# Attention and token mixing: the second batch in written order, with all sums of weights in it

## The chip, the cores and the metric

The kernel runs on one core of a Trainium2 chip. The metric is the device time of one execution in microseconds; of several runs the median is taken. A core has five engines that each work through their own instructions in order: PE (matmuls into PSUM), DVE, ACT and POOL (element-wise work) and SP (here it only issues DMAs). An instruction waits on semaphores for what other engines or DMAs have to finish, and while it waits, nothing behind it on its engine runs.

## The reference, cut to what matters

The first half is a clustered attention over 4 batches, 8 heads, 768 positions and a head size of 64. Its result, one matrix x of 768 x 512 per batch, goes through a token-mixing layer:

```python
def _moe_ref(x, w_theta, w_tok_r, w_tok_i, w_ch):
    theta = x @ w_theta
    cos_t, sin_t = (np.cos(theta), np.sin(theta))
    zr = x * cos_t
    zi = x * sin_t
    yr = np.einsum('ts,bsd->btd', w_tok_r, zr)
    yi = np.einsum('ts,bsd->btd', w_tok_i, zi)
    y = yr + yi
    u = x + y
    return (u + np.maximum(u @ w_ch, 0.0)).astype(np.float32)
```

All is float32. The change touches the token mixing alone, with one exception in the attention's last part.

## The kernel before

**Precision.** Matmuls of the second half take each operand as a pair: a high part (a cast on ACT, `nc.scalar.copy` into a float32r tile) and a low part (the value minus its high part, on POOL or DVE). A product is three matmuls: high by high, high by low, low by high.

**Tiles and stages.** A batch has NT = 6 tiles of 128 tokens; n = 6 b + t counts them over all batches. For each tile: `theta_parts` (L931) loads columns of x and makes `xh`, `xl`; `theta_angle` (L940) does the 12 matmuls of the angle into `tp`; `theta_turn` (L947) reduces the angle on DVE (`rotation_reduce`, L662), takes its absolute value on ACT, and transposes a block of x into `xn` on DVE (`rotation_turn`, L651, which also loads the next block `xb`); two sines on ACT (L986 or L965); two products with `xn` on DVE; then the pair `z`.

**Two ways to mix.** Batches 0 and 1 (b < `PLAIN` = 2) use `mix` (L1018), the plain products with `w_r[t]`, `w_i[t]` into `y`. `z` tiles come from the pool `mz` with two buffers. Batches 2 and 3 use `mix_forms` (L1107): seven products of sums of `z` with sums of weights, in place of the plain ones. The 7 x 6 = 42 sums of weights are made on the chip by `make_forms` (L1048). For a tile t it loads the raw weights into `spares[0]` and `spares[1]`; for each of the seven, DVE adds two parts (five of the seven; two are a part as it is), ACT casts to the high half and POOL subtracts to the low half of one of only two buffers, `spares[2]` and `spares[3]`, and SP stores the buffer to DRAM (`w_f`). `load_forms` (L1069) brings the sums back into tiles where the plain weights lay (`PLACE`, L1044). `forms[0]` lies in the four `spares` and in parts of `w_r[0]`, `w_i[0]`.

**Channel layer.** `channel_plain` (L1176) follows each plain batch: `add_y` (L1148) adds `y` to x on DVE, splits it on ACT (`uh`) and POOL (`ul`), and 96 matmuls with `w_c` (L1165) give the output.

**Order.** Up to the end of the attention and from `begin` (L1229) on, `in_order` (L689) ties each engine's instructions to the order in which they are written. Between these two, which before holds all of batches 0 and 1, the compiler's scheduler orders each engine by the program's priority and its own timing. There the loop at L1203 runs, per tile, `theta` of n + 2 (`AHEAD`), `mix` of n, and five or six steps of `make_forms`. From batch 2 on the steps are written out by hand: `done` (products with `xn`), `angle`, `before` (parts), the mixing, `turn`.

`behind(x)` (L628) places an instruction after x on its engine. In the attention, units u = 0 to `NUT` - 1 = 191 each end in exponentials on ACT (`exps`, L481).

Of the kernel before, what the change touches and what calls it, by code (L numbers as in the profile page):

```python
# [9 lines left out]
F32 = mybir.dt.float32  # L10
# [31 lines left out]
def kernel(  # L42
# [218 lines left out]
    def f(ap):  # L261
        return ap.bitcast(F32)
# [218 lines left out]
    def exps(u, j):  # L481

        pi, a, i = split_u(u)
        s = st[pi]
        last_exp[0] = nc.scalar.activation(out=s["at", a, i][:, j], in_=s["sc", j], func=AF.Exp, scale=SCALE)  # L485

    def add_exps(u):
# [108 lines left out]
    def run(gen):  # L596
        for _ in gen:
            pass
# [16 lines left out]
        first.update(rab=rab, xn=xn)  # L615

    first, first_sin = {}, [None]

    def rotation_tiles(n, name):
        pool = ma[n % 2]  # L620
# [7 lines left out]
    def behind(x):  # L628
        return tc.issue_after(x.ins) if x is not None else nullcontext()
# [240 lines left out]
    def u_tile(name):  # L870
        return m2.tile([P, NCT, HS], F32R, tag="u", name=name, bufs=4)
# [24 lines left out]
    def late():  # L896

        for t in range(EARLY, NT):
            for w, x in ((w_r, "r"), (w_i, "i")):
                hi, lo = w[t]  # L900
                kept = u_tile("kept").rearrange("p c s -> p (c s)").bitcast(F32)[:, 0:S]
                nc.sync.dma_start(out=kept, in_=w_d[t, x])
                with behind(weights_after[0]):
                    nc.scalar.copy(out=hi, in_=kept)
                nc.gpsimd.tensor_tensor(out=lo, in0=kept, in1=f(hi), op=ALU.subtract)
            if t == NT - 2:
                yield
        for c in range(NCT):
            for gen in split_w(*w_c[c], w_ch[c * P:(c + 1) * P], DM, wt_pair, nc.gpsimd, CK):
                run(gen)  # L910
            yield
# [8 lines left out]
    def load_columns(n):  # L920

        b, t = divmod(n, NT)
        if 0 < b < B and n not in columns:
            columns[n] = mxs.tile([P, NCT, P], F32, tag="xs", name=f"xs{n}")
            with tc.issue_after(last_load[0].ins):
                nc.sync.dma_start(out=columns[n], in_=xT_d[b][:, :, t * P:(t + 1) * P])
# [4 lines left out]
    def theta_parts(n, eng, after=None):  # L931
        b, t = divmod(n, NT)
        load_columns(n + 1)
        xs = columns.pop(n) if b else xts[b][:, :, t * P:(t + 1) * P]
        turning[n] = xh, xl, xn, kk, rab = rotation_tiles(n, f"{b}_{t}")
        nc.scalar.copy(out=xh, in_=xs)
        with behind(after):
            eng.tensor_tensor(out=xl, in0=xs, in1=f(xh), op=ALU.subtract)

# [12 lines left out]
    def theta(b, t):  # L952
        n = b * NT + t
        late = n == AHEAD
        theta_parts(n, nc.vector, last_out[0] if late else None)
        theta_angle(n, last_rows[0] if late else last_mix[0] if n == AHEAD + 1 else None)
        theta_turn(n)
        xh, xl, xn, kk, rab, tp = turning.pop(n)
        rotate(b, t, rab, xn)
# [7 lines left out]
    def turned(n):  # L967

        xh, xl, xn, kk, rab, tp = turning.pop(n)
        b, t = divmod(n, NT)  # L970
        for x in (1, 0):
            nc.vector.tensor_tensor(out=rab[:, x], in0=rab[:, x], in1=xn, op=ALU.mult)  # L972
        keep_turned(b, t, rab)

    def keep_turned(b, t, rab):
        zs[b, t] = rab
        z_d[b, t] = dram.tile([P, 2, DM // 2], F32, tag=f"z{t}", name=f"zd{b}_{t}", bufs=2)
        nc.sync.dma_start(out=z_d[b, t], in_=rab[:, :, DM // 2:DM])
# [39 lines left out]
    def mix(b, t):  # L1018
        for d in range(NCT):
            for w, (zh, zl) in zip((w_r[t], w_i[t]), zs[b, t]):  # L1020
                for zz, ww in ((zh, w[0]), (zh, w[1]), (zl, w[0])):
                    first = t == 0 and w is w_r[0] and zz is zh and ww is w[0]
                    last = t == NT - 1 and w is w_i[t] and zz is zl
                    for c0, c1, lead in cuts(d):
                        last_mix[0] = nc.tensor.matmul(  # L1025
                            y_at(d, c0, c1), lhsT=zz[:, d * P:(d + 1) * P], rhs=ww[:, c0:c1],
                            start=first and lead, stop=last, skip_group_check=True)
# [19 lines left out]

    def make_forms():  # L1048

        for t in range(NT):  # L1050
            for x, k in enumerate("ri"):
                with behind(last_mix[0]):
                    nc.sync.dma_start(out=f(spares[x]), in_=w_d[t, k])
            part = [f(spares[x])[:, c:c + HS] for x in range(2) for c in (0, HS)]
            yield
            for x, m in enumerate(ORDER):
                to = spares[2 + (7 * t + x) % 2]
                hi, lo = to[:, 0:HS], to[:, HS:S]
                p, op, q = W_SUM[m]
                src = part[p]  # L1060
                if op is not None:
                    src = mzb.tile([P, 2, HD], F32, tag="zb", name=f"sum{t}_{m}").rearrange("p x n -> p (x n)")[:, 0:HS]
                    nc.vector.tensor_tensor(out=src, in0=part[p], in1=part[q], op=op)
                nc.scalar.copy(out=hi, in_=src)  # L1064
                nc.gpsimd.tensor_tensor(out=lo, in0=src, in1=f(hi), op=ALU.subtract)  # L1065
                nc.sync.dma_start(out=w_f[t][:, m - 1], in_=f(to))
                yield

    def load_forms(t, ms=ORDER):  # L1069
        for m in ms:  # L1070
            nc.sync.dma_start(out=f(forms[t][m]), in_=w_f[t][:, m - 1])
# [76 lines left out]
    def add_y(b, c0, c1):  # L1148

        xT, n = xts[b], c1 - c0  # L1150
        uh, ul = (u_tile(f"u{x}{b}_{c0}")[:, :, 0:n] for x in "hl")
        for d in range(NCT):
            x = xT[:, d, c0:c1]
            for n0, n1, _ in cuts(d, c0, c1):
                nc.vector.tensor_tensor(
                    out=xT[:, d, n0:n1], in0=y_at(d, n0, n1), in1=xT[:, d, n0:n1], op=ALU.add)
            nc.scalar.copy(out=uh[:, d, :], in_=x)
            nc.gpsimd.tensor_tensor(out=ul[:, d, :], in0=x, in1=f(uh[:, d, :]), op=ALU.subtract)  # L1158
        return uh, ul
# [9 lines left out]
    def channel_out(b, e, ch, cp):  # L1169
        c = slice(ch * HS, (ch + 1) * HS)  # L1170
        ot = m2.tile([P, HS], F32, tag="ot", name=f"ot{b}_{ch}_{e}", bufs=2)
        nc.vector.scalar_tensor_tensor(
            out=ot, in0=cp, scalar=0.0, in1=xts[b][:, e, c], op0=ALU.max, op1=ALU.add)
        nc.sync.dma_start(out=out[b, e * P:(e + 1) * P, c], in_=ot)

    def channel_plain(b):  # L1176
        us = [add_y(b, ch * HS, (ch + 1) * HS) for ch in range(2)]
        for x in range(2 * NCT):
            ch, e = divmod(x, NCT)
            cp = (mbank(f"cp{b}_{x}") if x < 2 else y[x - 2])[:, 0:HS]  # L1180
            channel_products(cp, e, us[ch], range(NCT))
            channel_out(b, e, ch, cp)

    def channel(b, us):
        EARLY_GROUPS = 5
# [13 lines left out]

    rotate(0, 0, first["rab"], first["xn"])  # L1200
    theta(0, 1)
    late_weights, new_forms = late(), make_forms()
    for n in range(PLAIN * NT):  # L1203
        b, t = divmod(n, NT)
        theta(*divmod(n + AHEAD, NT))
        if b == 0:
            weights_after[0] = splits[n + 1]
            next(late_weights, None)
        mix(b, t)
        if 0 < n < PLAIN * NT - 1 and t < NT - 1:  # L1210
            for _ in range(5 if b == 0 else 6):
                next(new_forms, None)
        if b == PLAIN - 1:
            if t == NT - 2:
                run(new_forms)
            if t > 2:
                load_columns(n + AHEAD + 2)
            if t == NT - 2:
                load_forms(0)
            if t > 2:  # L1220
                load_forms(t - 2)
        if t == NT - 1:
            channel_plain(b)
            load_x(b + 1)
    us = [u_tile(f"u{x}") for x in range(4)]
    forms[4] = {
        m: us[x // 2].rearrange("p c s -> p (c s)")[:, x % 2 * S:(x % 2 + 1) * S] for x, m in enumerate(ORDER)}
    four[0] = pm[1].tile([P, 512], F32, tag="bank", name="four")
    begin = len(nc.cur_bb.bb.instructions)  # L1229

    last = B * NT

    def before(n):
        if n < last:
            theta_parts(n, nc.gpsimd)

    def angle(n):
        if n < last:
# [7 lines left out]
    def done(n):  # L1246
        if n in turning:
            turned(n)

    before(PLAIN * NT + 2)  # L1250
    z = split_z(PLAIN, 0, 0)
    for b in range(PLAIN, B):
        for t in range(NT - 1):
            n = b * NT + t
# [99 lines left out]
```

## Time and profile before

| | us |
|---|---|
| runs, median of 3 (lowest, highest) | 833.58 (832.99, 835.40) |
| the profiled execution, its own time | 833.82 |
| its span, first to last instruction | 832.1 |
| PE busy in the span | 777.1 (93%) |
| DVE, POOL, ACT busy | 639.5, 564.4, 414.1 |
| mean granted clock of PE | 0.966 |

Times inside the profile count from the start of the span. A row of a timeline has start, duration, engine, source line, operation, output and inputs, and in brackets the idle time of the engine before it with what ended it. In a view of windows, each engine's busy time in a stretch is followed by the number of its instructions. PE is busy in most of the span, so the question for each stretch is whether PE is busy there, and if not, which chain of other engines and DMAs it waits for.

### The profile page before, as it was taken

To read this page: it belongs to the slowest core of one execution; us is meant where nothing else is said; L and a number is where in the kernel's file an instruction comes from. 1 tells how busy PE (TensorE), PEld (TensorE's weight loads), DVE (VectorE), ACT (ScalarE), POOL (GpSimd) and SP (SyncE) were. 2 spreads that over 40 slices of the span, in tenths; PEclk is the share of its full clock that TensorE was granted. 3 is DMA by queue.
4 is the path that set the end of the run, shared out by engine and by line. 5 is a ranking of instruction groups with operands and counts; after the bars stand their busy time and mean duration, and the time that the engine had idled before them with its cause. 6 is when DMAs were issued, how large, how long until landed. Compare 5 with 4: busy or idle time off the path is not lost. (4 is left out here: it accounts for less than half of the span.)

```text
span 832.1 us, 14509 instructions
## 1 busy us (share of the span) xinstructions
PE 777.1 (93%) x5316; PEld 572.7 (69%) x5316; DVE 639.5 (77%) x797; ACT 414.1 (50%) x835; POOL 564.4 (68%) x345
## 2 busy tenths in 40 slices
PE   8999999999999999999799998499987598899698
PEld 6656666566665666656556887398877497898597
DVE  7688999999999999998595897745584288558544
ACT  3567666676766766665454553624442143224220
POOL 3577988899999999889583866755466145325340
PEclk9999999999999999999899999699999599999899
DMA  3113333244333443425246666569998876439542
GB/s 135 40 59 110 123 99 107 87 161 145 125 99 129 159 146 126 127 96 191 104 122 179 180 188 194 173 227 299 301 351 308 282 213 173 134 133 288 149 170 77
DMA packets 115235, 135.38 MB, mean 163 GB/s; under 512 B 62226, under 2 KB 81308, under 8 KB 114780
## 3 DMA queue, kind: packets, MB, share of 16 engines
q1 hardware_dynamic: 115164, 134.45, 50.8%
q8 instruction: 42, 0.69, 0.3%
q14 instruction: 29, 0.24, 0.1%
HBM read 96.99 MB, written 37.33 MB: 161 GB/s over the span
## 5 line engine op out<-in xcount | busy, mean ns | idle before, releaser
L485 ACT ACTIVATE at<-sc 128x384 f32<-128x384 f32 x384 | 173.9, 493 | 97.9 <-PE m L409 70.6
L431 DVE TENSOR_REDUCE nm<-m 128x1 f32<-128x768 f32 x192 | 180.2, 947 | 29.7 <-PE m L409 24.1
L496 POOL TENSOR_TENSOR acc<-at,at 128x768 f32<-128x768 f32 x64 | 125.7, 1965 | 39.4 <-ACT at L485 37.4
L409 PE MATMUL m<-hk,hq 64*128 64x384 f32 x384 | 147.7, 385 | 0.2 <-DVE nm L431 0.2
L557 PE MATMUL av<-at,vt 128*64 128x384 f32 x768 | 145.8, 501 | 0.2 <-ACT xt L572 0.2
L496 POOL TENSOR_TENSOR acc<-acc,at 128x768 f32<-128x768 f32 x64 | 132.8, 2075 | 10.9 <-ACT at L485 8.8
L409 PE MATMUL m<-mk,mq 64*128 64x384 f32 x384 | 128.7, 336 | 0.1
L409 PE MATMUL sc<-hq,hk 64*128 64x384 f32 x384 | 117.8, 393 | 6.1 <-ACT at L485 6.1
L409 PEld LDWEIGHTS sc<-hq,hk 64*128 64x128 f32 x384 | 55.3, 184 | 68.1 <-issue 25.3
L409 PE MATMUL sc<-mq,mk 64*128 64x384 f32 x384 | 97.5, 336 | 0.0
L409 PE MATMUL sc<-hq,lk 64*128 64x384 f32 x384 | 97.3, 335 | 0.0
L409 PE MATMUL sc<-lq,hk 64*128 64x384 f32 x384 | 97.3, 336 | 0.0
L557 PEld LDWEIGHTS av<-at,vt 128*64 128x64 f32 x768 | 46.7, 136 | 59.0 <-issue 54.0
L409 PEld LDWEIGHTS m<-hk,hq 64*128 64x128 f32 x384 | 70.8, 184 | 2.0 <-DVE nm L431 1.4
L409 PEld LDWEIGHTS m<-mk,mq 64*128 64x128 f32 x384 | 71.4, 186 | 0.8 <-DVE mk L374 0.4
L500 DVE TENSOR_TENSOR acc<-acc,acc 128x768 f32<-128x768 f32 x30 | 63.5, 2118 | 0.0
L409 PEld LDWEIGHTS sc<-mq,mk 64*128 64x128 f32 x384 | 54.8, 185 | 0.0
L409 PEld LDWEIGHTS sc<-lq,hk 64*128 64x128 f32 x384 | 54.7, 187 | 0.0
L409 PEld LDWEIGHTS sc<-hq,lk 64*128 64x128 f32 x384 | 54.7, 186 | 0.0
L1099 POOL TENSOR_TENSOR zf<-rab,zf 128x512 fp32r<-128x512 f32 x12 | 16.3, 1355 | 53.8 <-ACT zf L1098 53.8
L1025 PE MATMUL y<-wr_hi,z 128*128 128x512 f32 (+1 forms) x192 | 50.3, 340 | 1.4 <-POOL z L993 1.1
L1065 POOL TENSOR_TENSOR ws<-sum,ws 128x384 fp32r<-128x384 f32 x30 | 34.4, 1150 | 24.6 <-ACT ws L1064 22.3
(222 smaller groups left out, 1779.1 us busy)
## 6 DMA issues: line engine op xcount, KB each, us to landing
wf<-ws SPq DMA_DIRECT2D x42, 384.0 KB
ws<-wf SPq DMA_DIRECT2D x20, 384.0 KB
vt<-in_v_dram SPq DMA_DIRECT2D x16, 384.0 KB
rb<-sd SPq DMA_DIRECT2D x32, 192.0 KB
xT_d<-xt SPq DMA_DIRECT2D x16, 384.0 KB
xb<-xT_d SPq DMA_DIRECT2D x96, 64.0 KB
out_dram<-ot SPq DMA_DIRECT2D x32, 192.0 KB
rawq<-in_qT_dram SPq DMA_DIRECT2D x15, 384.0 KB
```

The costliest lines, as they stand in the source:

```text
L409: nc.tensor.matmul(out, lhsT=stat[r, cols], rhs=mov[r, over], start=start, stop=stop)
L431: nc.vector.tensor_reduce(out=s["nm", a][:, j, i // 2:i // 2 + 1], in_=s["m", j][:, :, 0:HS], op=ALU.max, axis=AX.XY, negate=True)
L485: last_exp[0] = nc.scalar.activation(out=s["at", a, i][:, j], in_=s["sc", j], func=AF.Exp, scale=SCALE)
L496: last_acc[0] = nc.gpsimd.tensor_tensor(out=s["acc", a, x], in0=prev, in1=at, op=ALU.add)
L500: nc.vector.tensor_tensor(out=s["acc", a, 0], in0=s["acc", a, 0], in1=s["acc", a, 1], op=ALU.add)
L557: nc.tensor.matmul(s["av"][64 * j:64 * j + 64], lhsT=s["vt"][:, i, j, :], rhs=s["at", a, i][:, j], start=(i == 0), stop=(i == NT - 1))
L1025: last_mix[0] = nc.tensor.matmul(y_at(d, c0, c1), lhsT=zz[:, d * P:(d + 1) * P], rhs=ww[:, c0:c1], start=first and lead, stop=last, skip_g ...
L1065: nc.gpsimd.tensor_tensor(out=lo, in0=src, in1=f(hi), op=ALU.subtract)
L1099: nc.gpsimd.tensor_tensor(out=l_, in0=of, in1=f(h_), op=ALU.subtract)
```

## The change

The written order now begins after the first batch (`begin` is moved behind `channel_plain(0)` and `load_x(1)`). The first batch makes no sums. The second batch is written out in the manner of the later ones; all 42 sums stand in its first five steps, in halves of four and three sums, 3, 3, 2, 2, 2 and 0 halves a step. The raw weights of the next tile are loaded behind the last store of a tile. The forms of tiles 1, 2, 0 and 3 are loaded at other places, `turn` and the first `split_z` of batch 2 move between `add_y` and the channel products, and `xh` of tile n = 1 is placed behind an exponential of unit NUT - 13.

```diff
@@ exps
+        if u == NUT - 13:
+            gate[0] = last_exp[0]
         last_exp[0] = nc.scalar.activation(out=s["at", a, i][:, j], in_=s["sc", j], func=AF.Exp, scale=SCALE)
@@ theta_parts
-        nc.scalar.copy(out=xh, in_=xs)
+        with behind(gate[0] if n == 1 else None):
+            nc.scalar.copy(out=xh, in_=xs)
@@ turned
-        keep_turned(b, t, rab)
+        if b >= PLAIN:
+            return keep_turned(b, t, rab)
+        z = mz.tile([P, 2, 2, DM], F32R, tag="z", name=f"z{b}_{t}")
+        for x in range(2):
+            nc.scalar.copy(out=z[:, x, 0], in_=rab[:, x])
+            nc.gpsimd.tensor_tensor(out=z[:, x, 1], in0=rab[:, x], in1=f(z[:, x, 0]), op=ALU.subtract)
+        zs[b, t] = [(z[:, x, 0], z[:, x, 1]) for x in range(2)]
@@ make_forms
+        def load_raw_weights(t):
+            for x, k in enumerate("ri"):
+                nc.sync.dma_start(out=f(spares[x]), in_=w_d[t, k])
+
+        load_raw_weights(0)
+        yield
         for t in range(NT):
-            for x, k in enumerate("ri"):
-                with behind(last_mix[0]):
-                    nc.sync.dma_start(out=f(spares[x]), in_=w_d[t, k])
             part = [f(spares[x])[:, c:c + HS] for x in range(2) for c in (0, HS)]
-            yield
             for x, m in enumerate(ORDER):
...
                 nc.sync.dma_start(out=w_f[t][:, m - 1], in_=f(to))
-                yield
+                if x == 3:
+                    yield
+            if t < NT - 1:
+                load_raw_weights(t + 1)
+            yield
@@ channel_plain
-    def channel_plain(b):
+    def channel_plain(b, n=None):
         us = [add_y(b, ch * HS, (ch + 1) * HS) for ch in range(2)]
+        z = None
+        if n:
+            turn(n)
+            if b == PLAIN - 1:
+                z = split_z(PLAIN, 0, 0)
...
+        return z
@@ the loops
+    def HALVES(b, t):
+        return (3, 3, 2, 2, 2, 0)[t]
     late_weights, new_forms = late(), make_forms()
-    for n in range(PLAIN * NT):
+    for n in range(NT):
+        theta(*divmod(n + AHEAD, NT))
+        weights_after[0] = splits[min(n + 1, NT - 1)]
+        next(late_weights, None)
+        mix(0, n)
+    channel_plain(0)
+    load_x(1)
+    begin = len(nc.cur_bb.bb.instructions)
...
+    before(NT + 2)
+    next(new_forms)
+    for n in range(NT, PLAIN * NT):
         b, t = divmod(n, NT)
-        theta(*divmod(n + AHEAD, NT))
-        if b == 0:
-            weights_after[0] = splits[n + 1]
-            next(late_weights, None)
+        done(n + 1)
+        if t < NT - 1:
+            angle(n + 2)
+        before(n + 3)
+        if b == PLAIN - 1:
+            for x in {3: (1,), 5: (2, 0)}.get(t, ()):
+                load_forms(x)
+        for _ in range(HALVES(b, t)):
+            next(new_forms, None)
         mix(b, t)
-        if 0 < n < PLAIN * NT - 1 and t < NT - 1:
-            for _ in range(5 if b == 0 else 6):
-                next(new_forms, None)
-        if b == PLAIN - 1:
-            if t == NT - 2:
-                run(new_forms)
-            if t > 2:
-                load_columns(n + AHEAD + 2)
-            if t == NT - 2:
-                load_forms(0)
-            if t > 2:
-                load_forms(t - 2)
-        if t == NT - 1:
-            channel_plain(b)
+        if t < NT - 1:
+            turn(n + 2)
+        else:
+            angle(n + 2)
+            z = channel_plain(b, n + 2)
+            load_forms(3) if b == PLAIN - 1 else None
             load_x(b + 1)
```

`before`, `angle`, `turn` and `done` are the functions that before had from batch 2 on; `before` now takes DVE for `xl` where n < 12 and POOL from there on.

More of the change, by code (lines that the diff above doesn't have):

```diff
@@ L617 @@
     first, first_sin = {}, [None]
+    gate = [None]
     def rotation_tiles(n, name):
@@ L1201 @@
     theta(0, 1)
+    def HALVES(b, t):
+        return (3, 3, 2, 2, 2, 0)[t]
     late_weights, new_forms = late(), make_forms()
-    for n in range(PLAIN * NT):
-        b, t = divmod(n, NT)
+    for n in range(NT):
         theta(*divmod(n + AHEAD, NT))
-        if b == 0:
-            weights_after[0] = splits[n + 1]
-            next(late_weights, None)
-        mix(b, t)
-        if 0 < n < PLAIN * NT - 1 and t < NT - 1:
-            for _ in range(5 if b == 0 else 6):
-                next(new_forms, None)
-        if b == PLAIN - 1:
-            if t == NT - 2:
-                run(new_forms)
-            if t > 2:
-                load_columns(n + AHEAD + 2)
-            if t == NT - 2:
-                load_forms(0)
-            if t > 2:
-                load_forms(t - 2)
-        if t == NT - 1:
-            channel_plain(b)
[L1224 to L1228, printed above, removed]
+        weights_after[0] = splits[min(n + 1, NT - 1)]
[3 more added lines that the diff above has]
+    load_x(1)
     begin = len(nc.cur_bb.bb.instructions)
@@ L1234, in before @@
         if n < last:
-            theta_parts(n, nc.gpsimd)
+            theta_parts(n, nc.vector if n < PLAIN * NT else nc.gpsimd)
     def angle(n):
@@ L1248, in done @@
             turned(n)
-    before(PLAIN * NT + 2)
-    z = split_z(PLAIN, 0, 0)
+    before(NT + 2)
+    next(new_forms)
+    for n in range(NT, PLAIN * NT):
+        b, t = divmod(n, NT)
+        done(n + 1)
[7 more added lines that the diff above has]
+            next(new_forms, None)
+        mix(b, t)
+        if t < NT - 1:
[4 more added lines that the diff above has]
+            load_forms(3) if b == PLAIN - 1 else None
+            load_x(b + 1)
+    us = [u_tile(f"u{x}") for x in range(4)]
+    forms[4] = {
+        m: us[x // 2].rearrange("p c s -> p (c s)")[:, x % 2 * S:(x % 2 + 1) * S] for x, m in enumerate(ORDER)}
+    four[0] = pm[1].tile([P, 512], F32, tag="bank", name="four")
     for b in range(PLAIN, B):
```

## The prediction

> **What bounds the kernel now.** I read the page first (PE is busy in 93% of the span), then busy time by stretch, cut where the stages of the second half change: first batch's products, its channel layer, second batch, its channel layer, start of the third batch. Columns: stretch, its length, busy time (and count) of PE, PEld, DVE, ACT, POOL, then granted clock, DMA share, GB/s.
>
> ```profile
> 449.00:520.00 71.00, 68.93 (x372) 57.53 (x364) 61.11 (x71) 32.13 (x56) 45.88 (x32) 1.00 0.67 200
> 520.00:551.00 31.00, 20.01 (x96) 18.25 (x96) 18.59 (x29) 14.24 (x29) 23.59 (x21) 0.78 0.54 163
> 551.00:619.00 68.00, 68.00 (x368) 58.64 (x368) 41.48 (x66) 28.22 (x53) 33.37 (x29) 1.00 0.96 309
> 619.00:640.00 21.00, 18.89 (x103) 17.61 (x102) 10.63 (x16) 5.67 (x12) 16.33 (x16) 1.00 0.85 312
> 640.00:662.00 22.00, 8.47 (x25) 7.03 (x24) 8.47 (x14) 3.47 (x7) 3.35 (x3) 0.56 0.99 347
> ```
>
> Both stretches of `mix` are PE's own: 68.93 of 71 and 68.00 of 68 us. What the sums of weights cost there is hidden. The time that is lost lies at 520 and at 640. The timeline of PE shows the holes, with what ended them:
>
> ```profile
> 519.02 0.51 PE L1025 MATMUL y<-wi_hi,z 128*128 128x256 f32 x2
> 530.05 1.01 PE L1165 MATMUL cp<-uh,wch_hi 128*128 128x384 f32 x2 [10.52 <-ACT uh L1157]
> 622.45 0.62 PE L1165 MATMUL cp<-uh,wch_hi 128*128 128x384 f32 x2 [2.09 <-ACT uh L1157]
> 644.75 1.33 PE L1114 MATMUL four<-ws,zf 128*128 128x384 f32 x3 [4.25 <-DMA ws<-wf]
> 652.00 1.30 PE L1114 MATMUL y<-ws,zf 128*128 128x384 f32 x3 [4.95 <-DMA ws<-wf]
> 657.62 1.30 PE L1114 MATMUL y<-ws,zf 128*128 128x384 f32 x3 [4.33 <-DMA ws<-wf]
> 661.60 0.63 PE L659 MATMUL tp<-wth_hi,xh 128*128 128x512 f32 x1
> ```
>
> The holes after 640 wait for `forms[0]`, whose tiles are the four `spares`: they can't be loaded until the last sum has left them. And there is one hole far earlier, inside the attention, in the timelines of ACT and PE:
>
> ```profile
> 398.60 0.62 ACT L936 CAST xh<-xT 128x512 fp32r<-128x512 f32 x1 [6.35 <-DMA xT<-xT_d]
> 399.66 0.82 PE L409 MATMUL sc<-hq,hk 64*128 64x384 f32 x2 [5.00 <-ACT at L485]
> 400.00:410.00 10.00, 10.00 (x72) 6.32 (x73) 6.28 (x7) 4.57 (x11) 3.64 (x2) 0.81 0.25 82
> ```
>
> ACT's queue put `xh` of tile n = 1 ahead of the exponentials, and it stood there 6.35 us until `xT` had landed; PE stood 5.00 us for the exponentials behind it.
>
> Last, the chain of waits, and the totals of who waited for whom (us, times, longest). They say what a sum of weights costs, one after another:
>
> ```profile
> 546.63 2.71 DMA wf<-ws
> 549.41 0.52 ACT ws L1064
> 550.00 1.02 POOL ws L1065
> 551.04 3.05 DMA wf<-ws
> 554.19 0.52 ACT ws L1064
> ...
> ACT ws L1064 <- DMA wf<-ws: 59.7, 26, 6.5
> ...
> L1066 SPq DMA_DIRECT2D wf<-ws x42: 319/360/2436, 475.6 to 646.3; - x42
> ```
>
> There are two buffers (`spares[2]`, `spares[3]`). A buffer is cast into by ACT, subtracted into by POOL, stored by SP, and cast into again only when the store has landed: 549.41 to 554.19 is 4.78 us for one turn, 2.4 us a sum. In before the 42 sums have 171 us, 475.6 to 646.3, and ten of them are cast before `mix` of the first batch ends at 519.5.
>
> **The change part by part.** *The gate on `xh`, n = 1.* It goes behind the exponential of unit NUT - 13 = 179 of 192. 192 units in 449 us are some 2.3 us each, so that is near 420, 20 us after `xT` landed: the wait is gone, and the consumer, `tp` of n = 1, isn't due before the attention's end. Gain: the 5.00 us of the hole, and of the 10 us behind it at a clock of 0.81 some 1.9; what is late next are PE's own products (10.00 of 10 us busy in that row). I take **-6.5** (bounds -5.0 and -7.0).
>
> *First batch without sums.* Ten pairs of cast and subtraction and their stores leave 449 to 520. PE is busy there in all but 2 us, so: nothing. The hole after it is another matter:
>
> ```profile
> 519.85 0.51 ACT L1064 CAST ws<-ws 128x384 fp32r<-128x384 f32 x1 [1.54 <-DMA wf<-ws]
> 521.95 1.59 DVE L988 TENSOR_TENSOR rab<-rab,xn 128x512 f32<-128x512 f32 x2 [3.22 <-ACT rab L986]
> 505.78 1.08 PE L659 MATMUL tp<-wth_hi,xh 128*128 128x512 f32 x4
> 551.17 1.09 PE L659 MATMUL tp<-wth_hi,xh 128*128 128x512 f32 x4
> 725.38 0.51 PE L1165 MATMUL four<-u,wch_hi 128*128 128x384 f32 x2
> 742.02 1.08 PE L659 MATMUL tp<-wth_hi,xh 128*128 128x512 f32 x4
> ```
>
> DVE comes to `add_y` late since it stands for sines that stand behind a cast of a sum that stands for a store. In after the sums of the second batch's first step may start as soon as `tp` of n = 7 (505.78, ends 508.7) has freed `xh`, so eleven sums still mix with this channel layer; only the thetas of n = 8, 9 leave it. The hole lies between 2.1 (the like one at 622.45) and 10.5; I take 6. The channel layer takes 16.6 us at full clock (725.38 to 742.02) and took 21.1 after the hole (530.05 to 551.17); I take 19. `tp` of n = 8 fits in the hole.
>
> The Trainium skill, "TensorE: Matmul & The Clock Gate" (What's actually happening), says that the array falls to half its clock after an idle window of 3.4 us and needs 3.4 us of work to come back; by that a layer after a hole costs 1.7 us more than 16.6, and the sum below would be 1.4 us less. The trace agrees on the clock (0.56 and 0.78 above) but shows 4.5 us more, part of which are waits.
>
> *Second batch: all 42 sums in its first five steps, in written order.* Step n issues, on each engine in this order: products of n + 1 with `xn`, casts of `z` (n + 1), `angle` (n + 2), parts of n + 3, then 11, 10, 7, 7, 7, 0 sums, then `mix`, then `turn` (n + 2). So everything behind the sums on ACT (Abs, both sines, and the next `z`) waits for their stores, and PE waits for `z`. The first step's sums have room beside the first channel layer. But the second step's begin with the casts of `z` of n = 8, whose buffer is free only when `mix` of n = 6 is over; ACT stands there with all 31 other sums behind it. From here the sums are the path, not PE: a step of PE is 11.2 us (from these two rows), and 31 sums in five steps of it would be 1.8 us each.
>
> ```profile
> 573.48 1.08 PE L659 MATMUL tp<-wth_hi,xh 128*128 128x512 f32 x4
> 584.63 1.08 PE L659 MATMUL tp<-wth_hi,xh 128*128 128x512 f32 x4
> ...
> 549.41 0.51 ACT L1064 CAST ws<-ws 128x384 fp32r<-128x384 f32 x1 [6.47 <-DMA wf<-ws]
> 564.01 0.51 ACT L1064 CAST ws<-ws 128x384 fp32r<-128x384 f32 x1 [0.23 <-DMA wf<-ws]
> ...
> 522.82 0.48 SPq L1053 DMA_DIRECT2D ws<-wd2r  x1
> 528.14 0.84 DVE L1063 TENSOR_TENSOR sum<-ws,ws 128x384 f32<-128x384 f32 x1 [0.78 <-DMA ws<-wd2r]
> ...
> 629.13 0.32 SPq L1066 DMA_DIRECT2D wf<-ws  x1
> 631.51 0.52 ACT L1064 CAST ws<-sum 128x384 fp32r<-128x384 f32 x1 [2.20 <-DMA wf<-ws]
> ```
>
> Seven casts span 14.6 us (549.41 to 564.01, the best seven of the trace), and the last one's cast and subtraction add 1.6. Then comes a thing that before didn't have: the raw weights of the next tile are now issued behind the last store on SP, so nothing hides them. Two issues of 0.4 and 0.5, a landing of up to 5.3 us (522.82 to 528.14) and a DVE sum make 4.6 to 6.8; I take 5.5, since the steps' sines and `z` run in the same time. One weight tile: 14.6 + 1.6 + 5.5 = 21.7 us.
>
> The sum, in times of before: `mix` of n = 5 ends 519.5; hole 6, layer 19, `mix` of n = 6 8.3 (11.2 less 2.9 of `tp`): 552.8. Two `z` and one `xh` at 0.62: 554.8. Three sums of tile 1 (two gaps of 2.43, and 1.6): 561.3. Four tiles of 21.7: 648.1. `load_forms(1)`, 2.75 MB on SP ahead of tile 4's stores, is 7.9 us at 347 GB/s, half of it beside the raw load: 652.1. Sines, `add_y` and the first `uh`: 3.5. Layer 19: 674.6. The first products of the third batch, 3.6 by these rows of the chain:
>
> ```profile
> 716.33 0.44 PE four L1114
> 716.77 3.14 PE y L1114 x18
> ```
>
> 678.2, where before was there at 661.6: **+16.5**. `forms[0]` has arrived by then (5.5 MB from 652, 16 us), so the three holes of before (13.5 us) are inside this figure as a gain.
>
> *The rest.* `forms[3]`, `x` and `forms[4]` now are all issued after the second channel layer, 7 MB that before had moved earlier; that is 20 us of a full queue (347 GB/s) where PE needs `forms[3]` only three steps on, but `xb` and `zb` stand behind them: **+2** (0 to 8). `xl` of n = 12, 13 goes from DVE to POOL: beside the channel layer, nothing; 1.3 us each if POOL is late there.
>
> Sum: 833.8 (the profiled execution; median of the runs 833.6) - 6.5 + 16.5 + 2 = 845.8; I say **845**.
>
> **The rivals.** *The sums keep pace (faster).* The place is the landing of a store. The shortest is 2.4 us (629.13 to 631.51); then a turn is 4.05 us, seven casts span 12.2, and the path has 4 x 2.4 + 0.8 = 10.6 us less. A lighter queue speaks for it: 551 to 619 ran at 309 GB/s, after would need some 21 MB in 99 us, 210. With a hole of 2.1, layers at 17 and `forms[1]` hidden: 10.6 + 3.9 + 4 + 4 = 22.5 less, **823**. It decides from 14 us saved. Against it: in before no seven casts did better than 14.6. By the Trainium skill, "DMA: Bandwidth & Descriptors" (Anatomy of one DMA), a transfer costs 2.0 us and its bytes at 436 GB/s, 2.9 us for these 384 KB, and this rival would then save 6 us less; the 2.4 above is shorter than that, so I let it stand.
>
> *The queue fills (slower still).* With the queue full the sums went at half the pace:
>
> ```profile
> L1065 POOL TENSOR_TENSOR ws<-sum,ws 128x384 fp32r<-128x384 f32 x11 | 11.9, 1083 | 18.0 <-ACT ws L1064 15.7 <-DVE kk L666 2.2
> L1065 POOL TENSOR_TENSOR ws<-ws,ws 128x384 fp32r<-128x384 f32 x5 | 5.1, 1016 | 14.3 <-ACT ws L1064 14.3
> ```
>
> That is 16 in 551 to 619, 4.25 us each. If the last two tiles go so, behind `forms[1]`, they take 29.8 instead of 21.7 each: **861**, and with the 8 of the rest 867.
>
> *The order does nothing but the gate works.* If the sums were hidden, PE alone would set the second batch and only the gate and holes would show: about 805. The 31 sums in 56 us speak against it; no chance worth naming.
>
> **How the numbers follow.** The chain of sums sets the second batch, 837 to 865: 0.52. The sums keep pace or nearly: 0.35, of which 0.25 end below 831 and 0.10 within 831 to 836, where this kernel's measurement can't tell (0.3%). The queue fills: 0.13. So faster 0.25, same 0.10, slower 0.65. The bounds taken together (hole, layers, span, raw load, forms) reach from -27 to far above; not all fall one way, so the range is 824 to 869.
>
> **What would show it.** Gate: no ACT wait for `xT` near 399 and no PE hole there. Sums: after the end of `mix` of n = 6, ACT's casts a steady 2.4 us apart within a tile, 6 to 8 between tiles, the wait for the store their releaser; PE holes of about 10 us each ahead of `mix` of n = 9, 10, 11 that wait for `z`. Third batch: no hole for `ws<-wf`. I am wrong if PE runs through the second batch without those holes, or if the hole at 520 stays at 10 and more.

## The result, and the profile after

The changed kernel takes 868.25 us (median of three runs, 866.02 to 870.56), the one before 833.58: a ratio of 1.0411, 95% interval 1.0361 to 1.0462. It is slower, inside the range, but by 34.7 us where 11.4 were forecast. Its profiled execution took 868.25 us, its span is 866.2 us.

Busy time by stretch of the changed kernel, cut at its own stages (columns as in the prediction): products of the first batch, its channel layer, the second batch in four pieces, its channel layer, the third batch up to its channel layer, the rest.

```profile
443.00:511.00 68.00, 68.00 (x367) 58.01 (x363) 51.41 (x71) 32.80 (x54) 37.38 (x26) 1.00 0.53 142
511.00:535.00 24.00, 20.17 (x97) 19.49 (x97) 10.50 (x20) 8.45 (x17) 16.82 (x15) 0.86 0.34 129
535.00:568.00 33.00, 33.00 (x179) 28.22 (x177) 12.04 (x16) 6.89 (x13) 10.58 (x9) 1.00 0.69 227
568.00:626.00 58.00, 13.45 (x61) 10.98 (x60) 22.29 (x30) 16.18 (x31) 24.69 (x23) 0.64 0.64 215
626.00:655.00 29.00, 25.42 (x121) 21.21 (x121) 12.29 (x20) 11.41 (x22) 15.82 (x15) 0.90 0.56 187
655.00:674.00 19.00, 18.89 (x97) 18.17 (x97) 9.37 (x18) 6.55 (x13) 11.73 (x11) 0.91 0.99 334
674.00:762.00 88.00, 68.98 (x323) 59.79 (x323) 55.38 (x91) 26.79 (x47) 34.43 (x27) 0.94 0.78 238
762.00:866.00 104.00, 93.24 (x494) 88.22 (x493) 60.09 (x107) 26.08 (x45) 32.99 (x27) 0.97 0.50 163
```

Two rows are to be seen. From 568 to 626 PE works 13.45 of 58 us, and no other engine and not the DMAs (share 0.64) are full either: a chain of waits. From 674 to 762 PE works 69 of 88 us. The timeline of PE, holes of the second batch, with what ended them:

```profile
586.79 2.07 PE L662 MATMUL tp<-wth_hi,xh 128*128 128x512 f32 x4 [18.67 <-ACT xh L940]
...
626.17 2.05 PE L662 MATMUL tp<-wth_hi,xh 128*128 128x512 f32 x4 [26.05 <-DVE rab L670]
654.71 2.21 PE L1181 MATMUL cp<-uh,wch_hi 128*128 128x384 f32 x4 [3.42 <-ACT uh L1173]
```

And the timeline of ACT: the gated `xh`, and the fifth and sixth weight tile's casts (L1076):

```profile
409.48 0.61 ACT L940 CAST xh<-xT 128x512 fp32r<-128x512 f32 x1
...
610.80 0.98 ACT L1076 CAST ws<-sum 128x384 fp32r<-128x384 f32 x2 [3.19 <-DVE sum L1075]
621.75 0.51 ACT L1076 CAST ws<-sum 128x384 fp32r<-128x384 f32 x1 [9.96 <-DMA wf<-ws]
...
630.07 0.51 ACT L1076 CAST ws<-sum 128x384 fp32r<-128x384 f32 x1 [2.81 <-DMA wf<-ws]
630.49 0.62 ACT L673 ACTIVATE rab<-rab 128x512 f32<-128x512 f32 x1
...
633.21 1.14 ACT L981 CAST z<-rab 128x512 fp32r<-128x512 f32 x2 [0.81 <-DVE rab L976]
634.25 0.61 ACT L940 CAST xh<-xs 128x512 fp32r<-128x512 f32 x1
638.15 0.98 ACT L1076 CAST ws<-sum 128x384 fp32r<-128x384 f32 x2 [3.29 <-DVE sum L1075]
...
650.60 0.51 ACT L1076 CAST ws<-sum 128x384 fp32r<-128x384 f32 x1 [2.81 <-DMA wf<-ws]
```

`xh` waits for nothing now. A weight tile takes ACT 12.45 us from its first cast to its last (638.15 to 650.60), 19.3 where a store stood behind `forms[1]` (9.96); behind the last cast come Abs, the sines, `z`, `xh`, and 8.1 us later the next tile's first. These are the steps that the prediction described. Two of its signs came out otherwise: within a tile the casts don't come a steady 2.4 us apart but in turns of about 1 and 3 (2.1 on average), and PE has two holes, 18.67 and 26.05 us, where three of about 10 were named. Both stand ahead of the angle matmuls of a step (those of n = 9 and 10) and wait for `xh` and for DVE's reduction, not for `z`; on ACT and DVE these stand behind sums as well.

Where the time went, by ends of stages. The middle column is the first experiment, the kernel before with nothing but the gate:

| us | before | gate alone | after |
|---|---|---|---|
| mix of the first batch starts | 449.7 | 443.5 | 443.1 |
| first channel layer ends | 551.3 | 546.6 | 534.6 |
| second channel layer ends | 637.7 | 631.8 | 674.0 |
| third batch's channel layer starts | 725.4 | 716.2 | 762.2 |
| span | 832.1 | 823.8 | 866.2 |

Against the gate alone the change gains 12.0 us up to the first channel layer, loses 54.2 in the second batch (85.2 to 139.4), loses 3.8 behind it (84.4 to 88.2) and gains 3.6 at the end.

### The profile page after: what moved, and what is told of

Its sections match the earlier page's. It is cut to its first block, busy times and chain, and to the rows that moved or that the text cites. A ratio compares the mean times of both kernels' runs of the same rounds, so it can differ in the third digit from the quotient of the medians.

```text
span 866.2 us, 14530 instructions
## 1 busy us (share of the span) xinstructions
PE 779.8 (90%) x5316; PEld 574.7 (66%) x5316; DVE 627.6 (72%) x795; ACT 416.6 (48%) x835; POOL 564.4 (65%) x347
## 4 chain that ended last, share of the span: by engine, by line
PE 51%; DMA 16%; DVE 11%; issue 7%; POOL 6%; ACT 5%; SPq 4%; ACTq 0%; DVEq 0%; POOLq 0%
PE sc L409 22%; PE av L559 14%; DMA wf<-ws 6%; PE m L409 3%; DMA xb<-xT_d 3%; PE y L1181 3%; SPq L650 2%; POOL ws L1077 2%; POOL zf L1115 2%; DMA zd<-rab 2%; PE lg L285 1%; DVE rab L976 1%; PE y L1130 1%; PE sm L526 1%; DMA out_dram<-ot 1%
## 5 line engine op out<-in xcount | busy, mean ns | idle before, releaser
L431 DVE TENSOR_REDUCE nm<-m 128x1 f32<-128x768 f32 x192 | 180.2, 947 | 26.1 <-PE m L409 20.9
L662 PE MATMUL tp<-wth_hi,xh 128*128 128x512 f32 x96 | 30.3, 442 | 56.0 <-DVE rab L670 32.1
L1077 POOL TENSOR_TENSOR ws<-sum,ws 128x384 fp32r<-128x384 f32 x30 | 30.7, 1032 | 57.1 <-ACT ws L1076 48.6
L662 PEld LDWEIGHTS tp<-wth_hi,xh 128*128 128x128 f32 x96 | 19.2, 210 | 61.6 <-issue 27.2
L1076 ACT CAST ws<-sum 128x384 fp32r<-128x384 f32 x30 | 15.1, 513 | 84.6 <-DMA wf<-ws 52.4
L409 PEld LDWEIGHTS sc<-lq,hk 64*128 64x128 f32 x384 | 54.2, 185 | 0.0
```

Of the source, the lines that this page charges most:

```text
L409: nc.tensor.matmul(out, lhsT=stat[r, cols], rhs=mov[r, over], start=start, stop=stop)
L431: nc.vector.tensor_reduce(out=s["nm", a][:, j, i // 2:i // 2 + 1], in_=s["m", j][:, :, 0:HS], op=ALU.max, axis=AX.XY, negate=True)
L662: nc.tensor.matmul(tp, lhsT=xx[:, c, :], rhs=w_th[c][k], start=(n == 0), stop=(n == 3 * NCT - 1))
```

## The experiments

All were compared with the kernel before on the same chip (830 to 832 us there), so ratios are to be set beside the changed kernel's 1.0411.

**The gate alone.** The kernel before with the lines on `gate` in `exps` and `theta_parts`, and nothing else.

> The kernel before with nothing but the gate on xh of tile n = 1. If the gate is worth what the start of mix of the first batch shows in the changed kernel (449.71 to 443.09), the time falls by 6.6 us, to about 827; ACT has no wait for xT near 399 and PE no hole of 5 us there. If instead part of those 6.6 us came from the rest of the change (the sums that left the first batch), the gate alone gives less than 5. If the time that the gate saves is lost again behind (the hole at 520, the wait for forms[0]), the end moves by less than the start of mix.

825.01 us, ratio 0.9926 (0.9898 to 0.9953), 6.1 us less. No hole near 400. The profile still has the one ahead of the first layer:

```profile
525.24 1.01 PE L1169 MATMUL cp<-uh,wch_hi 128*128 128x384 f32 x2 [10.80 <-ACT uh L1161]
```

So the gate is worth its 6 us all the way to the end, and the 12 us up to the first channel layer belong to the sums that left the first batch: 8 by this hole and one of 0.9 us behind it (in the changed kernel 2.2, 0.3 and 1.3 us stand in their place), most of the rest by `z` that no longer stands behind sums. The run with part of the sums back, below, bears this out.

**Eight store buffers instead of two.**

```diff
-                to = spares[2 + (7 * t + x) % 2]
+                k = 7 * (t - 1) + x
+                if t == 0:
+                    to = spares[2 + x % 2]
+                else:
+                    if k % 2 == 0:
+                        pair[0] = u_tile(f"wsu{k}").rearrange("p c s -> p (c s)")
+                    to = pair[0][:, k % 2 * S:(k % 2 + 1) * S]
```

> The changed kernel with the sums of tiles 1 to 5 written into the tiles of the pool of u (eight halves) in place of spares[2] and spares[3]; the first tile's seven sums as they were. Theory 1 (the sums wait for the landing of the store two sums back, and everything behind them on ACT waits with them): within a tile the casts come 0.9 to 1.2 us apart in place of 2.1, seven casts span some 6 to 7.5 us in place of 12.4, the holes of PE at 587 and 626 (18.7 and 26.1 us) lose some 20 us together, the whole comes to about 848. Theory 2 (the bytes of the stores and loads set the pace): the span stays at 12 us, and the time within 2 us of 868. Theory 3 (the raw weights' load behind the last store and the written order behind it, 8 us a tile, are what costs): the spans shrink but the gaps between tiles grow by what they shrink; 860 or more.

1.0140 (1.0088 to 1.0192); it was run once more for its profile:

> The run with eight halves of the tiles of u as store buffers once more, for its profile. Theory 1: within a tile (second tile on) seven casts span 6 to 8 us in place of 12.4, none waits for the landing of a store; the raw load behind the last store, some 8 us a tile, is unchanged, and PE's two holes are some 22 us shorter together.

1.0129 (1.0096 to 1.0161), some 23 us less than the changed kernel. ACT's timeline, a whole tile, and the next tile's first cast; then PE's holes:

```profile
592.11 0.98 ACT L1084 CAST wsu<-sum 128x384 fp32r<-128x384 f32 x2 [3.19 <-DVE sum L1083]
...
598.07 0.51 ACT L1084 CAST wsu<-sum 128x384 fp32r<-128x384 f32 x1 [1.23 <-DVE sum L1083]
...
611.98 0.98 ACT L1084 CAST wsu<-sum 128x384 fp32r<-128x384 f32 x2 [7.17 <-DVE sum L1083]
```

```profile
573.64 2.07 PE L662 MATMUL tp<-wth_hi,xh 128*128 128x512 f32 x4 [8.44 <-ACT xh L940]
599.51 2.04 PE L662 MATMUL tp<-wth_hi,xh 128*128 128x512 f32 x4 [12.66 <-DVE rab L670]
```

Seven casts take 6.0 us in place of 12.4, none waits for a store, and the two holes are 21.1 us in place of 44.7. The landing of the store two sums back was what set the pace within a tile. From tile to tile it is still 9 to 14 us (598.07 to 611.98 here, with the issue of `forms[1]` between).

**Raw weights a tile ahead, too.** In addition, the raw weights alternate between two pairs of `spares` and are issued before a tile's stores:

```diff
+        def raw(t):
+            return spares[2:4] if t and t % 2 == 0 else spares[0:2]
...
+            if 0 < t < NT - 1:
+                load_raw_weights(t + 1)
```

> The kernel with sums in the tiles of the pool of u, and the raw weights alternating between spares[0:2] and spares[2:4], loaded a tile ahead from the third tile on. Theory 1 (what is left of the holes in the second batch is the raw load behind the last store): the holes of PE ahead of mix of n = 9 and 10 are under 6 us together, and the time is some 8 us under that of the run without this (843), about 834. Rival (written order, the sines and z behind the sums, holds PE whatever the loads do): no more than 3 us are saved, 840 or over.

829.79 us, 0.9988 (0.9960 to 1.0016): another 1.4%, some 12 us. One hole of 11.95 us is left. So the raw load behind the last store was the second term, more than I had put down for this run.

**The sums left out, all bytes kept.** Four casts fill the two buffers once (the expectation says two), and then come only the 42 stores, the raw loads and the loads of `forms`; DVE's sums are left out as well:

```diff
...
-                nc.scalar.copy(out=hi, in_=src)
-                nc.gpsimd.tensor_tensor(out=lo, in0=src, in1=f(hi), op=ALU.subtract)
+                if t == 0 and x < 2:
+                    nc.scalar.copy(out=hi, in_=part[0])
+                    nc.scalar.copy(out=lo, in_=part[1])
```

> The changed kernel without the sums of weights: two casts fill the two buffers once, and the 42 stores, the raw loads and all loads of forms stay, so every byte is moved; the 40 other casts, all subtractions and the additions of DVE are left out, and what is stored as sums isn't sums. Theory 1 (the wait for each landing, with ACT, DVE and POOL in written order): the holes of PE at 587 and 626 are gone (45 us), the second channel layer ends at about 630 in place of 674, the time is about 825. Theory 2 (bytes, the DMA queues full): the holes stay at half or more, the time is 845 or over.

815.92 us, 0.9828 (0.9789 to 0.9866). The holes are gone (first row: the whole second batch), so the bytes by themselves don't hold the second batch. The second layer ends at 615.1, 59 us earlier than in the changed kernel. But to the third batch's channel layer it is then 94.5 us, the longest of all runs, and in the second row the DMA share is only 0.41: SP stands for the layer's output stores, with `forms[3]` queued behind them.

```profile
528.00:595.00 67.00, 66.34 (x358) 56.70 (x356) 25.00 (x36) 16.83 (x29) 14.07 (x11) 1.00 0.92 306
620.00:630.00 10.00, 5.90 (x15) 4.38 (x15) 3.13 (x7) 0.00 (x0) 0.00 (x0) 0.56 0.41 142
```

**Part of the sums back in the first batch.** `next(new_forms)` behind each `mix(0, n)` and `HALVES` of 2, 2, 1, 1, 1, 0.

> The changed kernel with the raw weights' first load and five of the twelve halves of sums (18 of 42 sums) made in the first batch, one half per tile after the first; the second batch's steps make 2, 2, 1, 1, 1, 0 halves. If the placing of all sums in the second batch is what costs, the holes of PE in the second batch (18.7, 26.1 us) fall to under 10 us together, mix of the first batch is at most 2 us longer, and the time falls by some 30 us, to about 838. If the written order itself costs (whatever the number of sums in a step), the holes lose less than half and the time stays over 855.

851.98 us, 1.0259 (1.0217 to 1.0302): less than half of the gain that was expected. PE's timeline: in the first batch `z` is late again and the hole of 10 us ahead of the first layer is back; in the second batch 11.52 and 5.72 are left of 44.7.

```profile
505.85 0.62 PE L1035 MATMUL y<-wr_hi,z 128*128 128x512 f32 x2 [1.00 <-ACT z L1001]
507.98 0.61 PE L1035 MATMUL y<-wr_hi,z 128*128 128x512 f32 x2 [1.16 <-POOL z L1003]
527.05 1.01 PE L1181 MATMUL cp<-uh,wch_hi 128*128 128x384 f32 x2 [9.52 <-ACT uh L1173]
...
597.89 2.08 PE L662 MATMUL tp<-wth_hi,xh 128*128 128x512 f32 x4 [11.52 <-ACT xh L940]
616.33 2.05 PE L662 MATMUL tp<-wth_hi,xh 128*128 128x512 f32 x4 [5.72 <-DVE rab L670]
```

The first layer ends 14.8 us later than in the changed kernel, the second batch gets 30 us shorter. Wherever sums go through two buffers, something on the same ACT queue pays.

**Another place in the written order.** The halves of a step behind its `mix` and `turn`, in place of ahead of them.

> The changed kernel with the halves of sums of a step placed behind mix and turn of that step in place of ahead of them; two store buffers as in the changed kernel. If the place in the written order costs (Abs, both sines and the reduction of the angle stand behind the sums that they do not need), part of the 8 us between two tiles now lies beside the sums: each of the four tiles is 2 to 4 us shorter, the time 852 to 860. If the landing of stores and of the raw weights is all, the time stays within 3 us of 868.

876.92 us, 1.0562 (1.0535 to 1.0589), against the expectation: 1.5% slower than the changed kernel. Behind the first step the steps are about as long as before: `z` follows `z` after 20.5 and 25.5 us (592.23, 612.74, 638.21), in the changed kernel after 20.9 and 27.3 (585.08, 605.96, 633.21). `z` now follows the last sum of a tile at once, but the next tile's first sum still waits for its raw weights. What is lost is lost in the first step. There the sums now stand behind the Abs of n = 8, whose angle comes behind the first channel layer. ACT's timeline, first of this run, then of the changed kernel:

```profile
531.99 0.64 ACT L673 ACTIVATE rab<-rab 128x512 f32<-128x512 f32 x1 [18.29 <-DVE rab L671]
...
533.81 0.91 ACT L1076 CAST ws<-sum 128x384 fp32r<-128x384 f32 x2
...
561.03 1.13 ACT L981 CAST z<-rab 128x512 fp32r<-128x512 f32 x2
```

```profile
508.12 0.98 ACT L1076 CAST ws<-sum 128x384 fp32r<-128x384 f32 x2 [2.52 <-DVE sum L1075]
...
554.48 1.14 ACT L981 CAST z<-rab 128x512 fp32r<-128x512 f32 x2 [0.81 <-DVE rab L976]
```

The first sum is cast 25.7 us later, so the sums of this step no longer lie beside the first channel layer, and the next `z` comes 6.5 us later.

The same edit on the version with everything together (below) cost 2%:

> The kernel with everything together (826.8), and the sums of a step behind its mix and turn. Its steps in the second batch take 15 us, 9.6 of sums and 5.5 of reduction, sines and z one after the other. If they now lie side by side, the hole of PE at 582 to 594 (12 us) goes and the time falls to about 815; if the sums, now between the sines and z, delay z by as much, it stays within 3 us of 827.

843.81 us, 1.0165 (1.0138 to 1.0192). There too ACT stands 18.16 us for the Abs of n = 8, the first sum is cast at 536.25 in place of 507.31 and the next `z` at 562.48 in place of 549.07, and the later steps are about as long as without the edit. So neither run shows a gain from the place within a step; a version that moved the sums of the later steps alone was not run.

**The loads behind the second layer.** Three runs ask what holds the 88 us to the third batch's channel layer. First, `forms[3]` moved ahead of the layer:

```diff
-            z = channel_plain(b, n + 2)
             load_forms(3) if b == PLAIN - 1 else None
+            z = channel_plain(b, n + 2)
```

> The changed kernel with the loads of forms[3] issued ahead of the second channel layer in place of behind it (as in the kernel before). Theory 1 (the 78 us from the first products of the third batch to its channel layer, 64 in the kernel before, come from forms[3], x and forms[4] stacked on SP behind the last out store): the stage shrinks by 5 to 10 us, the time comes to about 860; the first products may lose 2 to 4 us of it to out stores that now stand behind 2.75 MB more. Rival (it is bytes, wherever they stand): the 78 us stay, the time within 2 us of 868.

1.0451 (1.0401 to 1.0500), no gain; the stage is 89.1 us. DVE's wait for an output store, 12.2 us in the changed kernel, grew to 19.3. Then the same with `nc.scalar.dma_start` for the output stores of this layer:

> As the run before, and the out stores of the second channel layer are issued by ACT in place of SP. Theory 1 (an out store stands behind the megabytes issued earlier on the same queue, and the two buffers of the layer's output then hold DVE and the first products): DVE's wait of 12 us for an out store near 660 falls under 4 us, the first products take some 4 us in place of 7.2, and SP issues x and forms[4] some 10 us earlier, so the stage falls to 64 to 68 us; the time is 852 to 856. Rival (16 DMA engines are full, whichever queue issues): out stores still land 10 us late, the time is that of the run before within 2 us.

1.0434 (1.0388 to 1.0481), the same again. The stores no longer stand on SP, but land no better in sum: the longest wait is 10.0 us and all six are 20.8, the total that the run before had in two. And ACT now stood 24.4 us at their issue, with the next `xh` behind it. The waits for DMAs (us, times, longest), first with SP, then with ACT as issuer:

```profile
DVE ot L1188 <- DMA out_dram<-ot: 20.8, 2, 19.3
```

```profile
ACT xh L940 <- DVE ot L1188: 24.4, 1, 24.4
...
DVE ot L1188 <- DMA out_dram<-ot: 20.8, 6, 10.0
```

The Trainium skill, "DMA: Bandwidth & Descriptors" (Issuing engines are not separate DMA queues), says that DMAs of all issuing engines run on the same 16 DMA engines and interleave; the equal sums of 20.8 us in these two rows fit that.

Third, 5.5 MB less: the loads of `forms[2]` and `forms[3]` left out.

> The changed kernel without the loads of forms[2] and forms[3] (14 of 384 KB, 5.5 MB; their tiles keep the plain weights, so the third and fourth batch use other numbers). From the end of the second channel layer to the start of the third batch's channel layer it is 88.2 us in the changed kernel and 84.9 in the one before. Bytes theory: this stage is set by the megabytes that can only be issued once the sums are done, so with 5.5 MB less (16 us at 347 GB/s) it falls to 70 to 76, its matmuls being 69 us; the time falls to some 853 to 856. Rival (the chain of one step, xs, xh, angle, sines, z, sets it, whatever is loaded): 84 or more, the time over 864.

853.63 us, 1.0292 (1.0257 to 1.0327). The stage falls from 88.2 to 74.8 us; up to it the kernel is 2.1 us shorter, and behind it as long (104.1 and 104.0):

```profile
671.90:746.80 74.90, 67.08 (x326) 60.06 (x325) 56.03 (x88) 26.98 (x47) 35.00 (x27) 0.93 0.79 230
```

So what this stage has above its matmuls is set by megabytes that wait in line behind the second layer. In the kernel before the same stretch is 87.6 us (637.7 to 725.4, and not the 84.9 of the expectation; the row is its nearest in whole us). Its DMA engines are full in the first 22 us of it, where its three holes lie (share 0.99 in the prediction's row from 640), so the same is likely there; no run took bytes out of that kernel to show it.

```profile
638.00:725.00 87.00, 68.60 (x321) 60.91 (x321) 54.49 (x86) 26.58 (x47) 34.60 (x28) 0.86 0.73 223
```

In fourteen of the kernels here, with the second layer ending anywhere from 631 to 682, it is 84 to 90 us. The exceptions are the run without sums, with 94.5, and the three in which bytes were left out of this line or moved ahead of it: this one, and two below (79.2, 79.5).

**Loads moved ahead.** Nine loads (3.5 MB), whose tiles are free by then, issued in the second batch's second and fifth step:

```diff
-            for x in {3: (1,), 5: (2, 0)}.get(t, ()):
-                load_forms(x)
+            for x in {1: ((0, ORDER[4:]),), 3: ((1,),), 4: ((2, ORDER[:6]),),
+                      5: ((0, ORDER[:4]), (2, ORDER[6:]))}.get(t, ()):
+                load_forms(*x)
```

On the changed kernel:

> The changed kernel with the nine loads of forms (3.5 MB) issued ahead, as in best4. There the DMA engines were full in the second batch and nothing was won; here their share is 0.64 in the second batch, so there is room. If bytes alone count, the stage behind the second layer falls from 88 to about 79 and the time by 6 to 10 us, to 858 to 862. If it counts that a store of a sum lands behind the megabytes issued ahead of it on the same queue (9.96 us once in the changed kernel, behind forms[1]), each such load ahead of sums costs the chain 3 to 7 us, the stage falls as much but the second layer ends 5 to 12 us later, and the time stays within 4 us of 868.

867.38 us, 1.0425 (1.0387 to 1.0463). The stage is 79.5 us, and the second layer ends 9.2 us later (683.15). The cast whose store stood behind 2.7 MB of loads waited 10.42 us, the one behind 2.3 MB 9.39, the like one without them 3.0. There is room in the DMA engines, but not in the chain.

**Everything together.** Eight buffers, raw weights ahead, `forms[3]` ahead of the layer, output stores by ACT (`best`); then DVE's sum written straight into the low half of the store buffer (`src = f(lo)`, `best3`); then the nine loads ahead on top (`best4`).

> All of these together: sums in eight halves of the tiles of u, raw weights a tile ahead, forms[3] ahead of the second channel layer, its out stores issued by ACT. If the steps add up: about 820, under the kernel before (831 on this chip). If the loads that come earlier now only meet the stores that come faster, it stays over 830.

> The kernel with everything together (826.8), in which DVE's sums from the second tile on no longer go through two small buffers but into the low half of the store buffer itself, where POOL then subtracts in place. If the two buffers hold DVE (waits of 1.2 us for the subtraction two sums back, 4.6 us where sums of two tiles meet), a step of the second batch falls from 15 to 12 or 13 us, the hole of PE at 582 to 594 from 12 to 3 to 6 us, and the time to about 819. If the sums, the reduction, the sines and z are serial whatever the buffers, 825 or over.

> The run before, and nine of the loads of forms (three of forms[0], six of forms[2], 3.5 MB, 10 us at 347 GB/s) issued in the second batch's second and fifth step, where their tiles are already free, in place of behind the last sum. Bytes theory: the stage from the end of the second channel layer to the next one, 84.5 us, falls to 75 to 79, and the time to 810 to 814. Rival (what is loaded earlier only takes the queue from stores and raw weights, and the second batch gets longer by as much): within 3 us of the run before.

0.9948 (0.9924 to 0.9971), 0.9950 (0.9927 to 0.9973), 1.0001 (0.9976 to 1.0027). In `best3` the hole fell from 11.96 to 6.48 us as expected of the two small buffers, and the time didn't move: the stage behind the layer went from 84.6 to 88.0. In `best4` that stage fell to 79.2, and the second layer ended 13.6 us later. The stretches show why; first `best3`, then `best4`:

```profile
545.00:575.00 30.00, 29.92 (x160) 25.54 (x160) 22.26 (x25) 14.45 (x28) 21.71 (x18) 1.00 0.98 319
575.00:605.00 30.00, 23.52 (x116) 19.78 (x115) 20.15 (x22) 13.88 (x27) 27.61 (x23) 0.89 0.95 337
605.00:637.00 32.00, 30.63 (x167) 28.14 (x165) 17.30 (x30) 9.55 (x18) 15.48 (x15) 1.00 0.96 347
620.00:637.00 17.00, 16.15 (x90) 15.34 (x88) 3.67 (x6) 1.26 (x3) 3.59 (x4) 1.00 1.03 397
```

```profile
545.00:575.00 30.00, 25.97 (x142) 22.13 (x140) 15.87 (x19) 11.79 (x22) 17.23 (x15) 0.98 0.97 328
```

Once the buffers are out of the way, the DMA engines are nearly full (last but one column) from 545 on, as they were from 551 to 619 in the kernel before (0.96), and a megabyte moved within that stretch gains nothing. What helps is to move sums, and with them their bytes, into the first batch; these two runs don't tell the one from the other:

> The kernel best3 with the raw weights' first load and five of the twelve halves of sums made in the first batch, all of them in eight halves of the tiles of u, raw weights always a tile ahead. If the bytes from 545 to 700 hold the kernel, 18 stores and three raw pairs (some 9 MB, 25 us at 347 GB/s) less there give 10 to 20 us: the time falls to 808 to 818. If the sums in the first batch delay z and the first channel layer as they did in early (13 us), it stays over 824.

> The same with three halves in the first batch. If bytes hold, about 60% of the gain of the run before, 815 to 821; if the hole ahead of the first channel layer (9.5 us in early) comes from sums that stand late in the first batch, this one doesn't have it, and it is the better of the two.

820.88 us, 0.9880 (0.9840 to 0.9920), and 823.25, 0.9906 (0.9874 to 0.9937). With five halves of sums in the first batch (through the eight buffers) PE has no hole in the second batch, 67.00 of 67 us:

```profile
520.00:547.00 27.00, 19.02 (x96) 18.36 (x97) 16.22 (x32) 11.22 (x24) 18.64 (x18) 0.81 0.29 112
547.00:614.00 67.00, 67.00 (x362) 57.65 (x361) 46.08 (x60) 28.89 (x55) 44.36 (x36) 1.00 0.92 296
```

But the hole ahead of the first layer is back (9.18 us, within the first row), as the second expectation had it, so the gain is 1.2% and not 2. With three halves it is small, and the second batch keeps a hole of 2.49. Both beat the kernel before and the changed one; over the gate alone (0.9926) their lead is within the intervals.

## Why the prediction was right, and where it was wrong

| step | forecast | measured |
|---|---|---|
| gate | -6.5 | -6.1 alone; mix starts 6.6 earlier |
| first batch without sums | 0 | -2.7 |
| hole and first layer | 25 | 24.4 |
| mix of n = 6 ends (with the gate) | 546.3 | 545.8 |
| first sum of the second step | 548.3 | 556.0 |
| from there to the start of the second layer | 100.8 | 98.7 |
| second layer | 19 | 19.3 |
| its end to the third batch's channel layer | 69.4 | 88.2 |
| from there to the end | 106.7 | 104.0 |

*The mechanism was right, and shown*: the chain of sums took the place of PE in the second batch, by the landing of stores (eight buffers: 23 us) and the raw load behind the last store (another 12).

*The step that failed* is the last one, the stretch from the second channel layer to the third batch's: the first products of the third batch at 3.6 us, and "the rest" at +2 (0 to 8). It is 18.8 of the 22 us by which the span was missed. `forms[0]` had indeed arrived, and the three holes of before went: from the layer's end to the angle of n = 15 it is 12.7 us (673.98 to 686.64) where before had 23.9 (637.7 to 661.6). But 3.6 were forecast. Of the 9 us more, the sum had left out the angle of n = 14 (2.8), and 5.4 are holes in which PE waits for DVE, which had stood 12.21 us for an output store. From the angle of n = 15 on it is 75.5 us where before had 63.8: not +2 but +11.8. The angles of n = 15 and 16 on PE, and what DVE and ACT waited for ahead of each:

```profile
676.65 1.02 DVE L1188 SCALAR_TENSOR_TENSOR ot<-y,xT 128x384 f32<-128x384 f32 x2 [12.21 <-DMA out_dram<-ot]
686.64 2.04 PE L662 MATMUL tp<-wth_hi,xh 128*128 128x512 f32 x4 [2.88 <-DVE rab L670]
699.41 0.62 ACT L940 CAST xh<-xs 128x512 fp32r<-128x512 f32 x1 [9.71 <-DMA xs<-xT_d]
700.09 2.07 PE L662 MATMUL tp<-wth_hi,xh 128*128 128x512 f32 x4 [5.28 <-ACT xh L940]
```

I had priced 7 MB behind the layer at 2 us since the third batch's first matmuls need little of them. But `xs`, `xb` and the output stores stand in line with them, and each step needs those: 5.5 MB less in the line make the stretch 74.8 us; `forms[3]` earlier, or output stores on another queue, leave it at 87 to 89. So the time of the holes came back a few us later, as other waits. The changed kernel's waits from 655 to 762:

```profile
ACT xh L940 <- DMA xs<-xT_d: 17.5, 4, 9.7
DVE ot L1188 <- DMA out_dram<-ot: 15.3, 3, 12.2
...
DVE xn L655 <- DMA xb<-xT_d: 9.2, 4, 5.2
DVE rab L670 <- DMA zd<-rab: 6.5, 1, 6.5
```

*Smaller terms.* The second step's sums didn't wait for the buffer of `z`, as I had put it, but for their own predecessors: eleven sums of the first step took from 508 to 552, since a store stood behind x (1.5 MB; the cast behind it waited 9.44 us) and raw weights behind output stores: +7.7. Seven casts span 12.4 us and not 14.6, the figure of my faster rival; the load of `forms[1]` (a tile of 19.3, 6.9 more, where 4 were added) and gaps of 8.1 between tiles in place of 7.1 gave most of that back. That 98.7 lies so near 100.8 is in part luck. The first batch without sums was worth 2.7 and not nothing; PE had idled 2 of 71 us there. What the 2.7 us at the end are stays open.

*The rivals.* "The sums keep pace" had the right turn of a buffer and the wrong sum. "The queue fills" had the right size (861 to 867) by the wrong place: not the sums were slowed by a full queue, but the stage behind them. The 2.9 us that the prediction sets beside "the sums keep pace" are given by the Trainium skill, "DMA: Bandwidth & Descriptors" (Anatomy of one DMA), for DMAs that GpSimd issues; here SP issues them, and the prediction's own rows show one of 2.4.

## What to carry to other kernels

Here the holes that waited for a DMA went and nothing was gained, since the bytes behind them were neither fewer nor earlier. Take the whole stage up to the next place where all engines meet, and compare it with its bytes, before a hole is counted as won. Work that waits for its own stores to land, in a queue that is in written order, makes everything behind it wait as well; count its buffers against the landing time before choosing its place; neither of the two other places tried here made up for too few of them. And a small store behind megabytes on the same queue pays for them: here a cast waited 9.4 to 10.4 us for a store behind 1.5 to 2.7 MB, 3.0 without them.

## What was not expected of the hardware

DVE stood up to 19.3 us for an output store of 192 KB where 8 MB had been issued ahead of it on the same queue, and still up to 10.0 us where ACT issued the store. The DMA engines moved more than the 347 GB/s that the prediction took as full: 397 GB/s over 17 us in `best3` (the last of its four rows above), when loads of 384 KB were under way and, toward the end, some output stores that ACT issued.
